# The first input tiles over two DMA queues, the turn of tile 1 and the parameter vectors in the opening of a fused scan and feed-forward kernel

## The chip, the core and the metric

The kernel runs on one core of a Trainium2 chip. The metric is the device time of one execution in microseconds (us). The core has five engines that run their own instruction streams and meet at semaphores: TensorE (PE, with its weight loads listed apart as PEld), VectorE (DVE), ScalarE (ACT), GpSimd (POOL) and SyncE (SP). Transfers between the device memory and the core's own memory are issued by SP or ScalarE and carried by 16 DMA engines.

## What is computed

```python
x  = A_x                       # 1 x 2048 x 512, bf16
xn = layernorm(x)
s  = S5(xn)                    # a complex diagonal recurrence over 2048 steps, 512 states
g  = silu((gelu(xn @ w_gate) * (xn @ w_up)) @ w_down)    # inner width 1376
out = x + s * g

# S5: Lam_bar = exp(exp(log_dt) * (Lambda_re + i Lambda_im))
#     h[t] = Lam_bar * h[t-1] + B_bar @ xn[t];  y = 2 Re(C h) + xn * Dskip
```

The three vectors `log_dt`, `Lambda_im` and `Lambda_re` (512 values each) give the rotation angles, the decay `rho` and the complex coefficients that are folded into C.

## The kernel before, in words

The 2048 rows are worked in four slabs of 512 rows, each of four tiles of 128 rows (tile m of slab s). For each slab: normalise, turn the rows so that the 512 features lie on partitions (`xnT`), multiply with `w_up` (wu) and `w_gate` (wg) and form gelu(gate) * up, turn that product (`at_t`), multiply with `w_down` (wd); beside it the scan: multiply with B, rotate, scan, rotate back, multiply with C. `y_tile` joins the two and writes the output.

The order of the work is not worked out at run time. Every piece of work is a numbered step, given with its engine, a planned cost and what it reads and writes (`Plan.add`, line 57); the tuple `ORDER` (line 21) lists all step numbers in the order in which they are emitted. The order of the steps of one engine in that tuple is the order in which that engine works; the planned costs and due times are left over from the planner that made it and do nothing in the kernel.

The opening, slab 0, is a special case. Three things are wanted early: x, the weights wu, and the three vectors.

- `load_x` (line 221) loads one tile of x, 128 rows of 1 KB, on SP's queue. Tiles 0, 1 and 2 come first, then the first 1024 columns of wu in four pieces by rows (`load_w`, k = 0 to 3), wu's last 352 columns, tile 3 of x, wg in two pieces, then wd's last rows, slab 1, Dskip. The issues on SP stand in this order. Behind them on SP come the DMA transposes (`dma_t4`, line 363, at L364; B, L237; `at_t`, L465) with wd's main load (L684) between them.
- The three vectors (lines 254 to 257) are loaded on ScalarE's queue, behind a dummy activation, into two small tiles `pv0` and `pv1`.
- `dummies` and `fill` (lines 296 to 303) are matmuls on constants, before any data are there: seven of 512 columns, then 256 columns at two places.
- `center(m)` (line 334) takes the mean of tile m and subtracts it. For tile 0 the sum is split: VectorE sums 384 columns (L341), ScalarE 128 (L339), and VectorE subtracts both (L343). For tiles 1 and 2 ScalarE sums (L347) and VectorE subtracts (L348).
- `head_t(m)` (line 305) turns a tile with four TensorE transposes (L313 for tile 0, L328 for tiles 1 and 2), and copies the result out of PSUM to `xcT` (in the buffer W): tile 0 in two halves, on VectorE (L319) and ScalarE (L321), tiles 1 and 2 in one copy on VectorE (L330).
- `up_rows(m, k)` (line 380) is the first product: for tile m and row block k of wu, two matmuls of 512 columns (L388) that add up over k in two PSUM banks. After k = 3 ScalarE scales the result by the rows' factor `rs` and takes it out (`out_up`, L398). `first_w` (line 406, L418) does the other products of slab 0.
- `stats`, `squares` and `rstd` (lines 277, 351, 285) find the factor `rs` of each tile; the power is taken on GpSimd (L292). `scale0` (line 355, L360 and L357) scales the turned-to-be rows; the DMA transposes of slab 0 read them.
- `parameters` (line 599) turns `pv0` and `pv1` with two small transposes (L603, L604), copies 12 columns out on VectorE (L606), then GpSimd takes the power dt (L607) and later rho (L611). `angles` (line 613) works out the angles on VectorE (L614 to L618) and sine and cosine on ScalarE (L619, L620). `coefficients` (line 703, L708 to L726) and `tables` (line 622, L639) follow on VectorE.

In the order before, TensorE's first steps are: dummies, fill, the turn of tile 0 in two halves, fill, the turn of tile 1, the two parameter transposes, then `up_rows` (0, 0), the turn of tile 2, (1, 0), (1, 1), (0, 1), (2, 0), (2, 1), (0, 2), (1, 2), (0, 3), (1, 3), (2, 2), (2, 3), and `first_w`. GpSimd's are: iotas and the identity, dt, the factors of tiles 1, 0, 2 and 3, a copy of the sine, rho, a copy of the cosine.

Of the kernel before, what the change touches and what calls it, by code (L numbers as in the profile page):

```python
# [80 lines left out]
def kernel(  # L81
# [18 lines left out]
    P = 128  # L100
# [37 lines left out]
    pv0, pv1 = sb("pv0", [4, P]), sb("pv1", [8, P])  # L138
# [82 lines left out]
    def load_x(m, end, landed):  # L221
        dma_sp(end, landed, lambda: nc.sync.dma_start(out=x_tok[:, m, :], in_=x_r[:, m, :]), [("x", 0, m)])

    W2 = CH[1][1]
    load_x(0, 1.12, 2.92)
    load_x(1, 1.59, 3.35)
    load_x(2, 2.06, 3.75)
    load_w("wu", 0, 1, 0, W2, 2.53, 5.1)
    load_w("wu", 1, 2, 0, W2, 3.0, 6.3)
    load_w("wu", 2, 3, 0, W2, 3.5, 7.4)  # L230
    load_w("wu", 3, 4, 0, W2, 4.0, 7.9)
    load_w("wu", 0, KT, W2, F, 4.5, 9.2)
    load_x(3, 5.0, 9.6)
# [71 lines left out]
    def head_t(m):  # L305
# [20 lines left out]
        def f():  # L326
            for k in range(KT):
                T.transpose(tp[:, k, :], xn[m][:, k * P : (k + 1) * P], ident[:])  # L328
# [516 lines left out]
```

## Time and profile before

| | us |
|---|---|
| median of 3 runs | 178.52 (178.51, 178.52, 178.72) |
| span of the profiled execution, first to last instruction | 176.3 |
| median less span | 2.2 |
| first product on wu (start) | 5.00 |
| first `first_w` product (start) | 10.39 |

The profile gives no time of its execution beside the span. Rows of the profile are read so: a timeline row has the start and the length in us, the engine, the line of the kernel, the operation, what it writes and reads, its shape and how many instructions were merged; in brackets the idle time before it and what ended it. A chain row has start, length, engine, tile and line. A DMA issue row has the tile, the queue, the count, KB each, and us from issue to landing. A row of a stretch has the stretch, its length, busy us and count of PE, PEld, DVE, ACT and POOL, the granted TensorE clock, the share of the DMA engines and GB/s.

### The profile page before, as it was taken

Reading aid. Unit: us, or ns where it says so; the run is one execution under the profiler, and the core shown is the slowest. Engines: PE = TensorE matmul, PEld = TensorE weight load, DVE = VectorE, ACT = ScalarE, POOL = GpSimd, SP = SyncE. Lnnn points to the kernel's source line nnn. Section 1 sums busy time; section 2 is a strip of 40 time slices with the busy share of each in tenths; the row PEclk is TensorE's granted clock in tenths of the full one; section 3 lists DMA queues with packets and bytes.
Section 4 is the critical chain, followed back from the end, with each engine's and each line's share of the span. In section 5 each row is a group of like instructions: output and inputs, shape, how many; then the busy total and the mean of one; then the engine's idle time right before and its main releaser. Section 6 shows DMA issues by size and latency. Waiting matters only on the chain.

```text
span 176.3 us, 2421 instructions
## 1 busy us (share of the span) xinstructions
PE 172.3 (98%) x847; PEld 82.3 (47%) x847; DVE 156.9 (89%) x252; ACT 123.5 (70%) x236; POOL 11.2 (6%) x25
## 2 busy tenths in 40 slices
PE   8999999999999999999999999999999999999992
PEld 2555454444454544444455454444444455444451
DVE  3859999999699984999979999899999999999764
ACT  6599979969999999799588845383058518482240
POOL 2660030000200000000040000000000000000000
PEclk9999999999999999999999999999999999999999
DMA  5999999998000809422000084194000007627112
GB/s 156 322 371 225 205 226 260 219 279 137 0 0 12 188 20 192 95 75 46 0 0 6 30 137 95 41 182 86 0 0 0 0 30 162 65 41 154 45 58 76
DMA packets 48355, 18.66 MB, mean 106 GB/s; under 512 B 40312, under 2 KB 47832, under 8 KB 48344
## 3 DMA queue, kind: packets, MB, share of 16 engines
q1 hardware_dynamic: 48320, 18.52, 48.8%
q8 instruction: 6, 0.10, 0.3%
q14 instruction: 5, 0.04, 0.1%
q10 hardware_dynamic: 24, 0.00, 0.0%
HBM read 6.46 MB, written 2.10 MB: 49 GB/s over the span
## 4 chain that ended last, share of the span: by engine, by line
PE 97%; DVE 1%; issue 0%; DVEq 0%
PE ring L449 32%; PE ring L481 22%; PE ring L547 16%; PE ybank L497 15%; PE ring L418 5%; PE ring L388 3%; PE ybank L418 2%; PE ring L299 1%; DVE yg L502 1%; PE ybank L299 1%; DVE junk L508 1%; PE ybank L328 0%; PE ring L303 0%; PE ring L313 0%; PE ring L603 0%
## 5 line engine op out<-in xcount | busy, mean ns | idle before, releaser
L449 PEld LDWEIGHTS <-xnT 128*128 128x128 bf16 x288 | 28.2, 98 | 28.4
L481 PE MATMUL ring<-wd,atT 128*128 128x512 bf16 (+1 forms) x176 | 39.3, 379 | 0.0
L449 PE MATMUL ring<-wg,xnT 128*128 128x512 bf16 (+1 forms) x144 | 31.6, 357 | 0.0
L449 PE MATMUL ring<-wu,xnT 128*128 128x512 bf16 (+1 forms) x144 | 31.3, 357 | 0.0
L547 PE MATMUL ring<-xnT,BT 128*128 128x512 bf16 x128 | 30.1, 379 | 0.0
L578 DVE TENSOR_TENSOR_SCAN Fs<-rho,ini,W 128x512 bf16<-128x512 f32 x24 | 29.7, 1271 | 0.1
L452 ACT ACTIVATE ub<-ring 128x512 bf16<-128x512 f32 (+1 forms) x36 | 19.2, 555 | 13.8 <-PE ring L449 13.7
L497 PE MATMUL ybank<-C,hst 128*128 128x512 bf16 x120 | 27.7, 379 | 0.0
L481 PEld LDWEIGHTS <-atT 128*128 128x128 bf16 (+1 forms) x176 | 17.2, 97 | 20.9
L549 ACT ACTIVATE U<-ring 128x512 bf16<-128x512 f32 x32 | 18.1, 599 | 7.5 <-PE ring L547 7.5
L452 ACT ACTIVATE gt<-ring 128x512 bf16<-128x512 f32 (+1 forms) x36 | 19.5, 556 | 3.7 <-PE ring L449 3.5
L497 PEld LDWEIGHTS <-hst 128*128 128x128 bf16 x136 | 13.3, 98 | 14.0
L484 ACT ACTIVATE g<-ring 128x512 f32<-128x512 f32 x16 | 9.4, 594 | 14.3 <-PE ring L481 14.2
L547 PEld LDWEIGHTS <-BT 128*128 128x128 bf16 x128 | 12.5, 97 | 14.8
L559 DVE TENSOR_TENSOR Q<-U,tab 128x4096 bf16<-128x4096 bf16 x8 | 18.3, 2289 | 0.9 <-ACT tab L646 0.7
L559 DVE TENSOR_TENSOR Q<-Fs,tab 128x4096 bf16<-128x4096 bf16 x8 | 18.3, 2288 | 0.1
L502 DVE TENSOR_TENSOR yg<-ybank,g 128x512 bf16<-128x512 f32 x15 | 10.2, 685 | 5.8 <-PE ybank L497 5.7
L763 ACT ACTIVATE junk<-x_tok 128x512 bf16<-128x512 bf16 x16 | 10.0, 632 | 1.2 <-DMA x_tok<-in_A_x_dram 1.2
L493 ACT ACTIVATE ybank<-sk 128x512 f32<-128x512 bf16 x15 | 9.1, 605 | 1.7 <-DVE yg L502 1.6
L768 ACT ACTIVATE xna<-x_tok,nb,rs 128x512 bf16<-128x512 bf16 x12 | 9.5, 812 | 0.0
L578 DVE TENSOR_TENSOR_SCAN Fs<-rho,W 128x512 bf16<-128x512 f32 x8 | 9.3, 1210 | 0.1
L458 DVE TENSOR_TENSOR at<-gt,ub 128x1024 bf16<-128x1024 bf16 x12 | 8.2, 683 | 0.0
(140 smaller groups left out, 169.7 us busy)
## 6 DMA issues: line engine op xcount, KB each, us to landing
x_tok<-in_A_x_dram SPq DMA_DIRECT2D x3, 512.0 KB, 4.6
out_dram<-ot SPq DMA_DIRECT2D x12, 128.0 KB, 1.8
wd<-in_B_w_down_dram SPq DMA_DIRECT2D x1, 1280.0 KB, 7.1
wu<-in_B_w_up_dram SPq DMA_DIRECT2D x4, 256.0 KB, 3.9
wg<-in_B_w_gate_dram SPq DMA_DIRECT2D x1, 864.0 KB
x_tok<-in_A_x_dram SPq DMA_DIRECT2D x4, 128.0 KB, 2.1
wg<-in_B_w_gate_dram SPq DMA_DIRECT2D x1, 512.0 KB, 6.0
wu<-in_B_w_up_dram SPq DMA_DIRECT2D x1, 352.0 KB, 5.3
```

Of the source, the lines that this page charges most:

```text
L418: T.matmul(ps[:, 0 : b - a], lhsT=lhs(k), rhs=wt[:, k, a:b], start=(k == 0), stop=(k == KT - 1))
L449: T.matmul(ps[:, 0 : b - a], lhsT=xnT[:, s % 2, m, k, :], rhs=wt[:, k, a:b], start=(k == 0), stop=(k == KT - 1))
L452: acts(b - a, lambda: act(out=dst[:, a:b], in_=ps[:, 0 : b - a], func=AF.Copy if up else AF.Gelu_apprx_tanh), [("bank", r)], [key], table= ...
L481: T.matmul(ps[:], lhsT=atT[:fs, k, m * P : (m + 1) * P], rhs=wd[:fs, k, :], start=(k == 0), stop=(k == NFT - 1))
L497: T.matmul(ps, lhsT=hst[s % 2][:, j // NPT, j % NPT, m * P : (m + 1) * P], rhs=C2[:, j // NPT, j % NPT, c0:c1], start=(j == 0 and not seed ...
L502: dve(w, lambda: V.tensor_tensor(out=yg[e][:, c0:c1], in0=ps, in1=g2[gi][:, b, c0:c1], op=ALU.mult), [key, ("g2", gi, b)], [("yg", e, c0)])
L547: T.matmul(ps[:], lhsT=BT[:, ri, k, pt * P : (pt + 1) * P], rhs=xnT[:, s % 2, :, k, :], start=(k == 0), stop=(k == KT - 1))
L549: acts(512, lambda q=q, ri=ri, ps=ps: act(out=U[ui][:, ri, q, :], in_=ps[:], func=AF.Copy), [("bank", r)], [("U", ui, q, ri)])
L559: dve(4096, lambda: V.tensor_tensor(out=Qf, in0=src.unsqueeze(1).to_broadcast(WQ), in1=table, op=ALU.mult), reads, ["Q"], rate=2.0)
L578: pl.add(DVE, 1.12 if s == 0 else 1.185, lambda ri=ri, q=q, pt=pt, first=first: V.tensor_tensor_scan(out=Fs[:, ri, q, :], data0=rho[:, pt ...
L763: acts(512, lambda i=i, fn=fn, sc=sc, m=m: act(out=junk()[:], in_=x_tok[:, s * M + m, :], func=fn, scale=sc, accum_out=sx[:, s, i, m : m + ...
L768: acts(512, lambda m=m: act(out=xn[m], in_=x_tok[:, s * M + m, :], func=AF.Identity, scale=rs[:, s, m : m + 1], bias=nb[:, s, m : m + 1]), ...
```

## The change

Loads. Of x's tiles 0 and 1, rows 0 to 63 are loaded on SP's queue and rows 64 to 127 on ScalarE's; tile 2 is loaded on ScalarE's queue whole. So wu k = 0 stands third on SP's queue and no longer fourth. The three vectors move from ScalarE's queue to SP's, behind wu k = 3 and ahead of wu's last columns; they land in one tile `pv` of 128 x 128, zeroed by VectorE first.

Tile 0. VectorE sums 320 columns and ScalarE 192; the centring is done in two halves.

Turns. The four transposes of tiles 1 and 2 write two PSUM banks, and their copies are split: VectorE takes the first half, ScalarE the second.

Parameters. One matmul of `pv` with 12 columns of the identity takes the place of the two transposes. In the code and in the order it stands later.

Order. TensorE: six dummies (seven before), fill, the turn of tile 0, fill, the turn of tile 1, `up_rows` (0, 0), (1, 0), (0, 1), the turn of tile 2, (1, 1), (2, 0), (2, 1), (0, 2), the parameters, (1, 2), (2, 2), (0, 3), (1, 3), (2, 3), then as before. GpSimd: the factor of tile 0, dt, the factors of tiles 1, 2 and 3, then as before. VectorE: the copy of the parameters stands behind tile 0's statistics, and the angles behind the scaling of tile 0, with tile 3's statistics between them. ScalarE: sum of tile 1, copy of tile 0, sum of tile 2, copies of tiles 1 and 2, the squares; sine and cosine both stand behind the first four `out_up`.

Output. Tiles 0 and 1 of the last slab are written with one transfer each instead of two.

The rest of `ORDER` is the same sequence with other numbers.

```diff
-    def load_x(m, end, landed):
-        dma_sp(end, landed, lambda: nc.sync.dma_start(out=x_tok[:, m, :], in_=x_r[:, m, :]), [("x", 0, m)])
+    def load_x(m, end, landed, p0=0, p1=P):
+        dma_sp(end, landed, lambda: nc.sync.dma_start(out=x_tok[p0:p1, m, :], in_=x_r[p0:p1, m, :]), [("x", 0, m)])
+    PH = P // 2
+    for m, p0, p1 in ((0, PH, P), (1, PH, P), (2, 0, P)):
+        if m < 2:
+            load_x(m, 1.0 + 0.25 * m, 2.6 + 0.3 * m, 0, PH)
+        dma(ACT, 0.4, 1.7, lambda m=m, p0=p0, p1=p1: A.dma_start(out=x_tok[p0:p1, m, :], in_=x_r[p0:p1, m, :]), writes=[("x", 0, m)], rank=900.0)
-    load_x(0, 1.12, 2.92)
-    load_x(1, 1.59, 3.35)
-    load_x(2, 2.06, 3.75)
...
+    dve(64, lambda: V.memset(pv[:], 0.0), writes=[("pv", i) for i in range(3)], rank=900.0)
...
     load_w("wu", 3, 4, 0, W2, 3.2, 6.8)
+    for i, v in enumerate((A_log_dt, A_Lambda_im, A_Lambda_re)):
+        dma_sp(3.6 + 0.4 * i, 6.0, lambda i=i, v=v: nc.sync.dma_start(out=pv[4 * i : 4 * i + 4, :], in_=v.rearrange("(k p) -> k p", p=P)), [("pv", i)])
     load_w("wu", 0, KT, W2, F, 4.9, 8.2)
...
-        bank, key = ybank[(m + 1) % 2], ("y", (m + 1) % 2)
-        tp = bank[:].bitcast(BF16)[:, 0:D].rearrange("p (k t) -> p k t", t=P)
+        banks = [(ybank[i], ("y", i)) for i in range(2)] if m == 1 else [(ring[2 + i], ("bank", 2 + i)) for i in range(2)]
+        tps = [b[:].bitcast(BF16)[:, 0 : D // 2].rearrange("p (k t) -> p k t", t=P) for b, _ in banks]
...
-        dve(512, lambda: V.tensor_copy(out=xcT[:, :, m * P : (m + 1) * P], in_=tp), [key], [("xcT", m, 0), ("xcT", m, 1)], rate=2.0, rank=310.0 - 20 * m)
+        dve(256, lambda: V.tensor_copy(out=xcT[:, 0:2, m * P : (m + 1) * P], in_=tps[0]), [banks[0][1]], [("xcT", m, 0)], rate=2.0, rank=310.0 - 20 * m)
+        acts(256, lambda: act(out=xcT[:, 2:4, m * P : (m + 1) * P], in_=tps[1], func=AF.Copy), [banks[1][1]], [("xcT", m, 1)], rank=310.0 - 20 * m)
...
-            c = 3 * P
+            c = 320
...
-        cuts = (0, HD) if (NS - 1, 0) <= (s, m) < (NS - 1, M - 2) else (c0,)
...
-            T.transpose(pt_ps[:, 0:4], pv0[:, :], ident[0:4, 0:4])
-            T.transpose(pt_ps[:, 4:12], pv1[:, :], ident[0:8, 0:8])
+            T.matmul(ybank[0][:, 0:12], lhsT=pv[:], rhs=ident[:, 0:12], start=True, stop=True)
...
-    dummies(7, 3)
+    dummies(6, 3)
```

More of the change, by code (lines that the diff above doesn't have):

```diff
@@ L137 @@
     C2 = sb("C2", [P, 2, NPT, D])
-    pv0, pv1 = sb("pv0", [4, P]), sb("pv1", [8, P])
+    pv = sb("pv", [P, P])
     Drow = sb("Drow", [P, D])
@@ L243 @@
     mhalf = small("mhalf", M)
-    tiny = small("tiny", 1)
     e_t = small("e_t")
@@ L251 @@
         early.append(dve(32, lambda i=i: V.memset(at[i][:, F:FP], 0.0), writes=[("atpad", i)], rank=900.0))
-    one = nc.const_aps.tensor(1.0, [P, 1], FP32)
-    first = [acts(1, lambda: act(out=tiny[:], in_=one, func=AF.Silu), [], ["tiny"], rank=910.0, not_before=0.72)]
-    for i, (t, v) in enumerate(((pv0[0:4, :], A_log_dt), (pv1[0:4, :], A_Lambda_im), (pv1[4:8, :], A_Lambda_re))):
-        first = [dma(ACT, 0.48, 1.7, lambda t=t, v=v: A.dma_start(out=t, in_=v.rearrange("(k p) -> k p", p=P)),
-                     writes=[("pv", i)], rank=900.0, not_before=0.8, after=first)]
     iota_i = sb("iota_i", [P, NBA], I32)
@@ L322, in head_t @@
             return
[L323 to L324 removed]
+        banks = [(ybank[i], ("y", i)) for i in range(2)] if m == 1 else [(ring[2 + i], ("bank", 2 + i)) for i in range(2)]
+        tps = [b[:].bitcast(BF16)[:, 0 : D // 2].rearrange("p (k t) -> p k t", t=P) for b, _ in banks]
         def f():
             for k in range(KT):
[L328 to L330 removed]
+                T.transpose(tps[k // 2][:, k % 2, :], xn[m][:, k * P : (k + 1) * P], ident[:])
+        pe(KT, P, f, [("xc", m, 0), ("xc", m, 1), "ident"], [key for _, key in banks])
+        dve(256, lambda: V.tensor_copy(out=xcT[:, 0:2, m * P : (m + 1) * P], in_=tps[0]), [banks[0][1]], [("xcT", m, 0)], rate=2.0, rank=310.0 - 20 * m)
+        acts(256, lambda: act(out=xcT[:, 2:4, m * P : (m + 1) * P], in_=tps[1], func=AF.Copy), [banks[1][1]], [("xcT", m, 1)], rank=310.0 - 20 * m)
     head, sums0 = [], []
@@ L342, in center @@
                                            accum_out=ma[:, 0:1]), [("x", 0, 0)], [("yg", 0, 0), ("ma", 0)], base=0.15, rank=400.0, after=early)
-            head.append(dve(512, lambda: V.tensor_scalar(out=xn[0], in0=x, scalar1=ma[:, 0:1], scalar2=mb[:, 0:1], op0=ALU.subtract, op1=ALU.subtract),
-                            [("x", 0, 0), ("ma", 0), "mb"], [("xc", 0, 0), ("xc", 0, 1)], rate=2.3, rank=400.0, after=head[-1:]))
+            for i in range(2):
+                hc = slice(i * HD, (i + 1) * HD)
+                head.append(dve(256, lambda hc=hc: V.tensor_scalar(out=xn[0][:, hc], in0=x[:, hc], scalar1=ma[:, 0:1], scalar2=mb[:, 0:1], op0=ALU.subtract, op1=ALU.subtract),
+                                [("x", 0, 0), ("ma", 0), "mb"], [("xc", 0, i)], rate=2.3, rank=400.0, after=head[-1:]))
             return
@@ L510, in y_part @@
         mg = s * TS + m * P
-        cuts = (0, HD) if (NS - 1, 0) <= (s, m) < (NS - 1, M - 2) else (c0,)
-        for lo, hi in zip(cuts, (*cuts[1:], c1)):
-            dma(SP, 0.35, 1.5, lambda lo=lo, hi=hi: nc.sync.dma_start(out=out_td[mg : mg + P, lo:hi], in_=ot[o][:, lo:hi]), [("ot", o, c0)], [("out", s, m, lo)], svc=(2, 0.4, 0.9))
+        dma(SP, 0.35, 1.5, lambda: nc.sync.dma_start(out=out_td[mg : mg + P, c0:c1], in_=ot[o][:, c0:c1]), [("ot", o, c0)], [("out", s, m, c0)], svc=(2, 0.4, 0.9))
     def y_tile(s, m):
@@ L599, in parameters @@
     def parameters():
-        pt_ps = ring[2][:].bitcast(BF16)
         def f():
-            T.transpose(pt_ps[:, 0:4], pv0[:, :], ident[0:4, 0:4])
-            T.transpose(pt_ps[:, 4:12], pv1[:, :], ident[0:8, 0:8])
-        pe(2, 60, f, [("pv", i) for i in range(3)] + ["ident"], [("bank", 2)])
-        dve(12, lambda: V.tensor_copy(out=pf[:], in_=pt_ps[:, 0:12]), [("bank", 2)], [("pf", 0), ("pf", 1)], rank=245.0)
+            T.matmul(ybank[0][:, 0:12], lhsT=pv[:], rhs=ident[:, 0:12], start=True, stop=True)
+        pe(1, 60, f, [("pv", i) for i in range(3)] + ["ident"], [("y", 0)])
+        dve(12, lambda: V.tensor_copy(out=pf[:], in_=ybank[0][:, 0:12]), [("y", 0)], [("pf", 0), ("pf", 1)], rank=245.0)
         pool(1.15, lambda: G.tensor_tensor(out=dt_[:], in0=e_t[:], in1=ldt, op=ALU.pow), [("pf", 0), "e_t"], ["dt"], rank=245.0)
@@ L654 @@
     fill(256, 3)
-    parameters()
     for m in range(1, M - 1):
@@ L660 @@
     stats(0)
-    angles()
     rstd(0, 1)
@@ L675 @@
             up_rows(m, k)
+    parameters()
+    angles()
     for m in range(M - 1):
```

16 lines of the change are left out of this document (9 added, 7 removed), and 46 rows, old and new, of the table ORDER.

## The prediction

> **What bounds the kernel now.** I read the page's busy shares first, then the chain of waits in order of time.
>
> ```profile
> span 176.3 us, 2421 instructions
> PE 172.3 (98%) x847; PEld 82.3 (47%) x847; DVE 156.9 (89%) x252; ACT 123.5 (70%) x236; POOL 11.2 (6%) x25
> ```
> ```profile
> 1.77 2.13 PE ring L299 x5
> ...
> 4.50 0.40 PE ybank L328 x4
> 4.90 0.11 PE ring L603
> ...
> 5.03 0.55 PE ring L388 x2
> ...
> 5.81 4.75 PE ring L388 x22
> ...
> 166.13 5.20 PE ybank L497 x24
> ```
>
> Columns of the chain are start, length, and what holds it. From 5.03 to 171.3 us every piece is TensorE and the next begins where the last ends. So the end of the kernel is the start of the first product plus fixed work, and the change is worth what it does to that start, unless it opens a hole later. The profiled span is 176.3 us; the median run is 178.52, so 2.2 us lie around the span, which the change doesn't touch. The timeline of TensorE gives instruction starts, which I use from here on:
>
> ```profile
> 5.00 0.59 PE L388 MATMUL ring<-wu,W 128*128 128x512 bf16 x2
> ...
> 5.65 4.91 PE L388 MATMUL ring<-wu,W 128*128 128x512 bf16 x22
> 10.39 1.36 PE L418 MATMUL ybank<-wu,W 128*128 128x352 bf16 x8
> ```
>
> The opening stage is 24 matmuls and the turn of tile 2. 22 of them take 10.39 − 5.65 = 4.74, so 0.216 each and 0.43 for a step of two; the turn takes 5.65 − 5.00 − 0.43 = 0.22. What decides 5.00? The timeline of the other engines, and the issues with their time from issue to landing (one query for each issue; x's tile 0, then wu's rows k = 0 to 3):
>
> ```profile
> 0.72 1.34 SPq L222 DMA_DIRECT2D x_tok<-in_A_x_dram  x3
> 2.11 2.33 SPq L213 DMA_DIRECT2D wu<-in_B_w_up_dram  x5
> ```
> ```profile
> x_tok<-in_A_x_dram SPq DMA_DIRECT2D x1, 128.0 KB, 2.1
> ```
> ```profile
> wu<-in_B_w_up_dram SPq DMA_DIRECT2D x1, 256.0 KB, 2.8
> ```
> ```profile
> wu<-in_B_w_up_dram SPq DMA_DIRECT2D x1, 256.0 KB, 3.3
> ```
> ```profile
> wu<-in_B_w_up_dram SPq DMA_DIRECT2D x1, 256.0 KB, 4.5
> ```
> ```profile
> wu<-in_B_w_up_dram SPq DMA_DIRECT2D x1, 256.0 KB, 4.8
> ```
> ```profile
> 2.85 0.55 DVE L341 TENSOR_SCALAR_CACHE_REDUCE yg<-x_tok 128x384 bf16<-128x384 bf16 x1 [1.82 <-DMA x_tok<-in_A_x_dram]
> ...
> 3.33 0.63 ACT L347 ACTIVATE junk<-x_tok 128x512 bf16<-128x512 bf16 x1
> ...
> 3.52 0.41 DVE L343 TENSOR_SCALAR xna<-x_tok,ma,mb 128x512 bf16<-128x512 bf16 x1
> ...
> 4.09 0.35 DVE L348 TENSOR_SCALAR xna<-x_tok,ma 128x512 bf16<-128x512 bf16 x1 [0.16 <-ACT junk L347]
> 4.36 0.28 DVE L319 COPY W<-ring 128x256 bf16<-128x256 bf16 x1
> ```
>
> SP issues one transfer each 0.46 us ((2.11 − 0.72) / 3). Tile 1 is issued at 1.18 and lands at about 3.3, where its sum on ScalarE starts (3.33); centring follows at 4.09, its turn at 4.50, the two parameter transposes, then the product. On the other side wu's first rows land at 2.11 + 2.8 = 4.9. **Two things end together at 5.00**: the turn of tile 1 with the parameters behind it, and the landing of wu k = 0. Later rows land at 2.58 + 3.3 = 5.9, 3.06 + 4.5 = 7.6 and 3.53 + 4.8 = 8.3. Their first users start at 6.08 (two matmuls after 5.65), 7.81 (ten) and 8.67 (fourteen): margins of 0.2 to 0.4 us.
>
> **The change, part by part.** *x in halves.* Tiles 0 and 1 go out as 64 rows on SP and 64 on ScalarE, tile 2 on ScalarE alone.
>
> ```profile
> 0.79 0.55 ACTq L256 DMA_DIRECT2D pv<-in_A_log_dt_dram  x1
> ```
>
> ScalarE's first issue starts 0.07 after SP's and holds its queue 0.55, so the upper half of tile 1 goes out near 1.34 against 1.18 for the whole tile now. A half on two queues is not in the trace. Bounds for landing: 0.2 us earlier (the data of half a tile), 0.2 later (ScalarE's later issue). I take tile 0 at 0.05 and tile 1 at 0.05 earlier. The split of tile 0's sum (320 columns on VectorE, not 384: 0.55 × 64/384 = 0.09 less) and the centring in two halves get tile 0 turned some 0.2 sooner, but its copy (L319) stays behind tile 1's centring on VectorE, which waits for ScalarE's sum: nothing is gained there. The memset of pv and the six instead of seven warming matmuls lie ahead of the data, in idle time (VectorE waits 1.82 before 2.85).
>
> *Turn of tile 1, then the product.* Both orders turn tile 1 first; what goes from between are the parameters. Turn at 4.45, plus 0.22: the product could start at T = 4.68. I take 4.70.
>
> *wu moves up one place on SP*, 0.46 earlier. But the same 640 KB have to pass before its first rows are in. A table of stretches shows how full the DMA engines are:
>
> ```profile
> 1.70:2.50 0.80, 0.80 (x4) 0.24 (x3) 0.00 (x0) 0.50 (x2) 0.19 (x1) 1.00 0.82 200
> 2.50:3.40 0.90, 0.90 (x4) 0.34 (x3) 0.55 (x2) 0.47 (x3) 0.00 (x0) 1.00 0.91 265
> 3.40:5.00 1.60, 1.60 (x15) 0.68 (x14) 1.25 (x6) 1.60 (x6) 0.00 (x0) 1.00 0.92 284
> 5.00:8.00 3.00, 3.00 (x19) 1.49 (x18) 2.53 (x11) 1.36 (x4) 2.10 (x5) 1.00 1.01 326
> ```
>
> The last two columns are the DMA share and GB/s. Until 5.0 a tenth or so lies open; after that nothing does. If x and wu ran at 326 from 1.7 on, 655 kB would take 2.0 us, against 2.6 to 2.7 at the three rates shown: bounds of 0 and 0.6 earlier. I take the middle, 0.3: rows land at 4.6, 5.6, 7.3 and 8.0.
>
> *The new order of products* is tile 0, 1, 0 (k = 1), turn of tile 2, tiles 1, 2, 2, tile 0 (k = 2), parameters, and the rest. Split copies (VectorE and ScalarE, a bank each) let a product follow its turn after one step of two: 0.28 for the copy against 0.43, hidden. One matmul of 12 columns for the parameters: between one transpose's 0.22/4 = 0.06 and the present 0.11; I take 0.06. The stage then ends at the latest of four: T + 24 × 0.216 + 0.22 + 0.06 = T + 5.46 = 10.16; wu k = 1, needed 0.86 after T, so 5.6 + 4.60 = 10.2; wu k = 2, needed 2.81 after T, so 7.3 + 2.65 = 9.95; and the parameters, needed 3.24 after T (7.94), so their landing + 2.22.
>
> *Parameters on SP behind wu k = 3.* They can't land before those rows' share on the same engines: as early as hidden (7.2), as late as 8.0 + 0.1. I take 8.0, which gives 10.22. wu's last columns and tile 3 are issued some 1 us later, behind three small issues; DMA share 1.01 says the queue is full then, so this is hidden; without that cover it would be that 1 us, less their margins.
>
> So the stage ends at **10.22 instead of 10.39: 0.17 us gained**.
>
> *What is late next.* The parameters also feed a chain on GpSimd and VectorE:
>
> ```profile
> 5.57 1.03 POOL L607 TENSOR_TENSOR dt__136<-e_t,pf 128x4 f32<-128x4 f32 x1 [3.68 <-DVE pf L606]
> ```
> ```profile
> 10.68 0.23 POOL L289 TENSOR_SCALAR ve<-mv 128x1 f32<-128x1 f32 x1 [1.14 <-DVE mv L281]
> 11.00 0.55 POOL L292 TENSOR_TENSOR rs<-ve,mhalf 128x1 f32<-128x1 f32 x1
> 11.51 0.29 POOL L627 CAST sh<-sbt 128x128 bf16<-128x128 f32 x1
> 11.76 1.11 POOL L611 TENSOR_TENSOR rho<-e_t,a 128x4 f32<-128x4 f32 x1
> ```
> ```profile
> 12.90 0.23 DVE L708 TENSOR_TENSOR nre<-rho,cbt 128x4 f32<-128x4 f32 x1 [0.90 <-POOL rho L611]
> ```
>
> Now dt starts at 5.57 and three scale factors follow in its slack. In the new order dt starts near 8.6 (matmul at 7.95, copy, then behind tile 0's factor), ends at 9.6, and tiles 1, 2 and 3 follow at about 0.9 each (10.68 to 11.55): 12.4 instead of 11.55. rho and the coefficients move with it: 12.90 becomes 13.8. VectorE already waits 0.90 there; I count no idle time behind it that would catch this up, so its tables come 0.9 late too. SP waits for tile 3's scaling before its transposes, and wd's load is queued behind them:
>
> ```profile
> 12.03 3.60 SPq L364 DMA_TRANSPOSE xnT<-xna  x2
> ...
> 22.37 0.93 SPq L684 DMA_DIRECT2D wd<-in_B_w_down_dram  x1
> ```
> ```profile
> wd<-in_B_w_down_dram SPq DMA_DIRECT2D x1, 1280.0 KB, 7.1
> ```
> ```profile
> 30.87 7.13 PE ring L481 x33
> ```
>
> wd lands at 22.37 + 7.1 = 29.5 and is used from 30.87 in the chain, which runs 0.16 behind the starts (5.81 against 5.65): 1.2 us of slack. 0.9 late and TensorE 0.17 early leaves 0.1 to 0.2. Hidden, barely. The output of two late tiles in one transfer instead of two isn't in the last tiles' path: nothing.
>
> Forecast: 178.52 − 0.17 = **178.35**.
>
> **The rivals.** *DMA fills at once (faster).* If halves on two queues close the open tenth, wu lands 0.5 to 0.6 earlier and T, with tile 1 at 3.1, is 4.5: the stage ends at 9.95 to 10.0, gain 0.4, 178.1. For: 0.82 and 200 GB/s at the start. Against: tile 1's upper half is issued later than the whole is now.
>
> *Parameters late (slower).* If wu k = 3 comes no sooner than 8.3 on the engines that carry the parameters, these land at 8.4: TensorE, in order, stands from 7.94, the stage ends at 10.62 (+0.23), dt starts at 8.9 or later and wd is 1.3 to 1.4 late, another 0.2 of stall: 178.9 to 179.0. It decides from a landing of 8.17 on, where the stage is no earlier than now. For: k = 2 and 3 need 4.5 and 4.8 us from issue, against 2.8 for k = 0; a full queue stands ahead of any small transfer. Against: only four of the engines' shares matter.
>
> *Halves buy nothing.* Both halves share the same engines; x lands as now or 0.1 later and wu k = 1 at 5.9, but it is needed 0.2 sooner in the new order: 5.9 + 4.60 = 10.5, 178.6. For: the DMA share is already 0.9.
> [...]
>
> *The clock.* Two fills in the timeline:
>
> ```profile
> 3.70 0.42 PE L303 MATMUL ring<-const-bfloat16-1.0 128*128 128x256 bf16 x1
> ...
> 4.23 0.27 PE L303 MATMUL ring<-const-bfloat16-1.0 128*128 128x256 bf16 x1
> ```
>
> The same matmul takes 0.42 and then 0.27; warming matmuls run at 2.13 / 5 = 0.43, products at 0.216. The pace doubles between 3.70 and 4.23, after 3 us of steady work. Six warming matmuls and the fill end near 3.5, and TensorE then idles 0.2 to 0.3 before the first turn. If that puts the doubling off by another 2 to 3 us past 4.7, half of it is lost: 1.0 to 1.5, 179.7. Against: the work also began only at 0.76.
> [...]
>
> **How the numbers follow.** Forecast 0.29 (0.23 within 0.2%, 0.06 faster); DMA fills at once 0.18 (0.16 faster, 0.02 within); parameters late 0.31 (0.25 slower, 0.06 within); halves buy nothing 0.14 (0.10 within, 0.04 slower); clock 0.08 slower. 0.2% is 0.36 us, about what a measurement of this kernel can tell from no change. Faster 0.22, same 0.41, slower 0.37. The range, 177.95 to 179.3, takes in the ends of the first four and leaves out the clock; the forecast alone is 178.1 to 178.6.
>
> **What would show it.** First product near 4.70 and not 5.00; k = 1 rows landing by 5.6; the first 352-column product near 10.2; dt at 8.6, coefficients at 13.8, wd's first use with no wait. I'm wrong if TensorE waits at the parameter matmul, if a second pace shows after 4.7, or if a hole opens between 18 and 35 us.

## The result and the profile after

The changed kernel takes 180.77 us (median of 14 executions, 178.60 to 181.34); the kernel before, beside it on the same chip, 178.65 (178.43 to 179.22, 14 executions). The ratio is 1.0084, 95% interval 1.0064 to 1.0104: by the medians **slower by 2.1 us** where 178.35 was forecast, outside the range. The ratios leave out executions more than 1.5% above the fastest of the same kernel (two of these fourteen, and four of ten when the kernel after ran again as e12, the profiled one among them), so that 1.0084 is 1.5 us where the medians differ by 2.1. Four of the fourteen took 178.60 to 179.46; the profile below is not of one of these, and what they were spared isn't known.

The head of the profiled execution (180.35 us):

```profile
span 178.6 us, 2409 instructions
...
PE 171.5 (96%) x829; PEld 81.8 (46%) x845; DVE 156.8 (88%) x254; ACT 124.0 (69%) x238; POOL 11.3 (6%) x25
```

TensorE is busy no longer than before (171.5 against 172.3) in a span that is 2.3 longer, so what was lost is time in which it stands idle. The timeline of TensorE shows the first part of that, its waits the second (columns of the waits: engine, what is waited for, us in all, times, longest):

```profile
4.27 0.54 PE L315 MATMUL ring<-ident,xna 128*128 128x128 bf16 x4 [0.58 <-DVE xna L348]
...
5.38 0.40 PE L330 MATMUL ybank<-ident,xna 128*128 128x128 bf16 x4 [0.46 <-DVE xna L353]
5.61 1.48 PE L393 MATMUL ring<-wu,W 128*128 128x512 bf16 x6
...
8.89 0.17 PE L604 MATMUL ybank<-ident,pv 128*128 128x12 bf16 x1
...
11.07 1.36 PE L423 MATMUL ybank<-wu,W 128*128 128x352 bf16 x8
```
```profile
PE ring L486 <- DMA wd<-in_B_w_down_dram: 1.2, 1, 1.2
```

The first product starts at 5.61 (5.00 before), the first product of 352 columns at 11.07 (10.39): **0.68 late**. Then wd is not there: a wait of 1.2 us; between the starts of the matmuls around it 1.4 us are missing. 0.68 + 1.4 is 2.1 of the 2.3; the rest are small waits. Which work stands behind both is in the chain of waits:

```profile
1.36 2.77 DMA x_tok<-in_A_x_dram
4.21 0.73 ACT junk L352 x2
4.97 0.36 DVE xna L353
5.38 0.40 PE ybank L330 x4
...
9.35 1.03 POOL dt__135 L607
...
11.26 0.61 DVE st L282
...
13.69 1.08 POOL rho L611
...
21.33 0.60 DVE at L436
...
23.81 1.16 SPq L470
25.02 7.96 DMA wd<-in_B_w_down_dram
33.02 2.10 PE ring L486 x9
```

Before, this chain ran on TensorE alone from 5.03 on. Now it starts with the upper half of x's tile 1 on ScalarE's queue (issued 1.36, landed 4.13), goes by way of its sum, centring and turn into the first product, and later leaves TensorE: dt, tile 3's statistics, rho, the tables, a transpose on SP, and wd's load behind it. The DMA issues of the first 12 us (columns: tile and queue, count, KB each, median us from issue to landing) and SP's timeline:

```profile
x_tok<-in_A_x_dram SPq DMA_DIRECT2D x2, 64.0 KB, 2.1
x_tok<-in_A_x_dram ACTq DMA_DIRECT2D x2, 64.0 KB, 2.8
x_tok<-in_A_x_dram ACTq DMA_DIRECT2D x1, 128.0 KB, 3.1
```
```profile
0.72 1.21 SPq L222 DMA_DIRECT2D x_tok<-in_A_x_dram  x2
1.98 2.00 SPq L213 DMA_DIRECT2D wu<-in_B_w_up_dram  x4
4.09 0.31 SPq L240 DMA_DIRECT2D pv<-in_A_log_dt_dram  x1
4.95 0.25 SPq L240 DMA_DIRECT2D pv<-in_A_Lambda_im_dram  x1
...
6.09 0.42 SPq L213 DMA_DIRECT2D wu<-in_B_w_up_dram  x1
...
9.26 1.12 SPq L686 DMA_DIRECT2D Drow<-in_A_Dskip_dram  x1
13.92 3.53 SPq L369 DMA_TRANSPOSE xnT<-xna  x2
...
25.02 0.73 SPq L684 DMA_DIRECT2D wd<-in_B_w_down_dram  x1
```
```profile
SPq L213 <- DMA wu<-in_B_w_up_dram: 0.5, 1, 0.5
SPq L240 <- DMA wu<-in_B_w_up_dram: 0.5, 1, 0.5
```

A half on SP takes as long to land as a whole tile did (2.1 us), the upper half of tile 1 on ScalarE's queue 2.8. SP now holds still inside the loads: the second parameter row until wu k = 0 has landed (4.93), wu's last columns until wu k = 1 has landed (6.07). The operands of the transfers in the trace show why: in both kernels they take turns on eight semaphores (S103 to S110), over both queues together, and each load that came to a semaphore again was issued after its last user, six to ten issues earlier, had landed (4.95 after 4.93, 6.09 after 6.07). Before, ten transfers stood ahead of wu's last columns, which shared a semaphore with x's tile 2 (landed 3.88) and didn't wait; now twelve do, and the partner is wu k = 1 (6.07). They go out at 6.09 instead of 4.01, and the last load, Drow, lands at 17.59 instead of 15.67. The DMA engines, at a share of 1.01 from 5.0 to 8.0 us before, are no longer full there:

```profile
5.00:8.00 3.00, 2.62 (x18) 1.28 (x19) 1.93 (x6) 1.88 (x6) 0.00 (x0) 1.00 0.81 258
```

Two theories came of this, and a third later. **F**: halves don't bring x sooner; each costs a longer issue (0.58 us on SP, 0.40 for a whole tile before) and lands like a whole tile. **D**: the two more transfers run into the eight semaphores, the loads end late, and what follows on SP, wd last of all, is late too. The rival to D, **P**: the parameters' later chain on VectorE and GpSimd holds SP up by itself. **G**: TensorE's idle stretches ahead of the first product decide when its full pace comes.

### The profile page after: what moved, and what is told of

Same layout as the page of the kernel before. It is cut to its first block, busy times and chain, and to the rows that moved or that the text cites. A ratio compares the mean times of both kernels' runs of the same rounds, so it can differ in the third digit from the quotient of the medians.

```text
span 178.6 us, 2409 instructions
## 1 busy us (share of the span) xinstructions
PE 171.5 (96%) x829; PEld 81.8 (46%) x845; DVE 156.8 (88%) x254; ACT 124.0 (69%) x238; POOL 11.3 (6%) x25
## 4 chain that ended last, share of the span: by engine, by line
PE 79%; DVE 8%; DMA 6%; POOL 2%; issue 1%; ACT 1%; SPq 1%; DVEq 0%; ACTq 0%
PE ring L454 31%; PE ring L486 21%; PE ybank L502 14%; PE ring L550 12%; DMA wd<-in_B_w_down_dram 4%; DVE st L282 2%; DMA x_tok<-in_A_x_dram 2%; DVE Q L639 1%; DVE yg L507 1%; PE ring L393 1%; SPq L470 1%; POOL rs L294 1%; DVE mv L283 1%; DVE tab L639 1%; POOL rho L611 1%
## 5 line engine op out<-in xcount | busy, mean ns | idle before, releaser
L552 ACT ACTIVATE U<-ring 128x512 bf16<-128x512 f32 x32 | 18.1, 599 | 7.5 <-PE ring L550 7.5
```

Source lines behind the costliest of these rows:

```text
L552: acts(512, lambda q=q, ri=ri, ps=ps: act(out=U[ui][:, ri, q, :], in_=ps[:], func=AF.Copy), [("bank", r)], [("U", ui, q, ri)])
```

## The experiments

All are the kernel after with the edit that the text gives; e6, e7 and e11 are the kernel before with one; e12 is the kernel after itself. The last five columns come from one execution of each. "Hole" is the time missing between the starts of the matmuls around wd's first use; Drow's landing is the end of the opening loads.

| kernel | median (range), executions | before beside it | ratio, 95% | span profiled | first product | first of 352 | wd lands | hole |
|---|---|---|---|---|---|---|---|---|
| e1_x_whole | 179.75 (178.93 to 180.12), 10 | 178.74 | 1.0061, 1.0041 to 1.0081 | 177.9 | 4.96 | 11.34 | 32.19 | 0.6 |
| e2_tile3_first | 180.20 (178.64 to 181.26), 10 | 178.74 | 1.0076, 1.0037 to 1.0115 | 179.5 | 5.83 | 11.39 | 33.40 | 1.2 |
| e3_halves_one_queue | 182.32 (181.4 to 183.3), 4 | 178.74 | 1.0213, 1.0144 to 1.0281 | 179.7 | 6.64 | 13.25 | 34.06 | 0.5 |
| e4_two_queues_whole | 180.15 (178.83 to 181.56), 4 | 178.74 | 1.0116, 1.0024 to 1.0208 | 177.0 | 5.53 | 10.97 | 31.30 | 0.1 |
| e5_loads_as_before | 178.96 (178.30 to 180.67), 10 | 178.79 | 1.0029, 0.9998 to 1.0060 | 176.9 | 4.88 | 10.91 | 30.72 | 0 |
| e6_only_halves | 183.44 (182.47 to 184.06), 4 | 178.79 | 1.0234, 1.0159 to 1.0309 | 181.2 | 7.58 | 15.05 | 32.80 | 0 |
| e7_three_more_loads | 179.22 (178.46 to 180.86), 10 | 178.79 | 1.0016, 0.9980 to 1.0053 | 176.7 | 5.07 | 10.48 | 30.75 | 0 |
| e8_wu0_ahead_of_x2 | 179.05 (178.62 to 180.43), 10 | 178.79 | 1.0012, 0.9977 to 1.0047 | 177.8 | 5.04 | 11.59 | 31.92 | 0.1 |
| e9_seven_fills | 179.26 (178.42 to 180.26), 8 | 178.53 | 1.0032, 1.0009 to 1.0056 | 178.5 | 5.63 | 11.35 | 32.65 | 1.0 |
| e10_no_parameter_loads | 179.66 (179.27 to 179.95), 4 | 178.53 | 1.0060, 1.0037 to 1.0083 | 177.9 | 5.62 | 11.09 | 31.81 | 0.45 |
| e11_six_fills | 178.52 (178.12 to 179.11), 10 | 178.53 | 1.0006, 0.9991 to 1.0021 | 176.6 | 5.37 | 10.78 | 30.38 | 0 |
| e12_after_again | 181.25 (178.84 to 182.51), 10 | 178.53 | 1.0097, 1.0058 to 1.0136 | 180.7 | 5.84 | 13.41 | 35.12 | 1.4 |
| e13_more_fills | 179.53 (178.92 to 180.88), 10 | 178.73 | 1.0043, 1.0019 to 1.0067 | 178.1 | 5.30 | 10.85 | 32.49 | 0.95 |
| e14_loads_before_tile3_first | 178.66 (178.22 to 179.19), 10 | 178.73 | 0.9990, 0.9958 to 1.0022 | 176.5 | 4.97 | 10.47 | 30.66 | 0 |
| e15_wd_early | 183.20 (182.27 to 184.39), 4 | 178.73 | 1.0246, 1.0191 to 1.0300 | 180.5 | 6.29 | 13.28 | 22.03 | 0 |

### The halves: e1, e3, e4, e6

e1 loads tiles 0 to 2 whole on SP and leaves the rest of the change:

```diff
-    for m, p0, p1 in ((0, PH, P), (1, PH, P), (2, 0, P)):
-        if m < 2:
-            load_x(m, 1.0 + 0.25 * m, 2.6 + 0.3 * m, 0, PH)
-        dma(ACT, 0.4, 1.7, lambda m=m, p0=p0, p1=p1: A.dma_start(out=x_tok[p0:p1, m, :], in_=x_r[p0:p1, m, :]), ...)
+    for m in range(3):
+        load_x(m, 1.0 + 0.25 * m, 2.6 + 0.3 * m)
```

> The changed kernel with x's tiles 0, 1 and 2 loaded whole on SP's queue again, in the order of before; all else as changed. Theory S (the second queue makes x late: in the changed kernel tiles 0 and 1 land at 3.14 and 4.13 us, before at 2.83 and 3.31): tiles land at 2.8, 3.3 and 3.9, the first product starts at 4.75 to 5.0 instead of 5.61, the first 352-column product at 10.3 to 10.5 instead of 11.07; the parameter chain starts 0.6 earlier, so wd's load too, and the hole of 1.5 us ahead of the down products shrinks to 0.5 to 0.9: 178.9 to 179.4. Rival C (the late parameters are all of the loss, the loads count for nothing): the hole stays at 1.5 us and the time above 180.3.

The first product is back at 4.96, so its 0.6 us belong to the way x is loaded (F). But wu k = 1 landed only at 6.72 in this execution, so that the first product of 352 columns came at 11.34, not at 10.5 or sooner, and the time is 179.75, above what was expected. The waits show both losses:

```profile
PE ring L393 <- DMA wu<-in_B_w_up_dram: 0.8, 1, 0.8
PE ring L486 <- DMA wd<-in_B_w_down_dram: 0.4, 1, 0.4
```

e3 puts both halves on SP's queue, and tile 2 too; e4 keeps two queues with whole tiles (0 and 2 on SP, 1 on ScalarE):

```diff
e3  +        load_x(m, 1.0 + 0.25 * m, 2.6 + 0.3 * m, p0, p1)      # upper half: SP as well
e4  +        if m != 1: load_x(m, ...)                             # whole
e4  +        else: dma(ACT, ..., A.dma_start(out=x_tok[:, m, :], in_=x_r[:, m, :]), ...)
```

> The changed kernel with the same halves of tiles 0 and 1, but all of x on SP's queue (lower half, upper half, tile after tile, then tile 2), nothing on ScalarE's. Theory S (the second queue is what makes x late): two more issues of about 0.4 us each stand ahead of tile 1 and wu; tile 0 lands at 2.9 to 3.1, tile 1 at 3.6 to 3.9, sooner than the 4.13 of the changed kernel; first product 5.0 to 5.4. Rival H (halving itself makes x late, small transfers moving as slowly on any queue): tile 0 at 3.2 or later, tile 1 at 4.1 or later, first product at 5.6 or later.

> The changed kernel with x in whole tiles, tile 1 on ScalarE's queue and tiles 0 and 2 on SP's. Theory S: with both queues issuing at once each issue takes 0.55 us or more (0.40 alone), and tile 1, though issued at 0.78, lands no sooner than 3.3, as it did third of a kind on one queue; tile 0 at 2.9 to 3.1; first product 4.8 to 5.2. Rival H (only halves are slow, two queues in themselves are a gain): issues of 0.40, tile 1 lands by 3.0, first product by 4.7 or held by wu alone.

SP's timeline in e3:

```profile
0.72 3.12 SPq L222 DMA_DIRECT2D x_tok<-in_A_x_dram  x5
3.89 1.85 SPq L213 DMA_DIRECT2D wu<-in_B_w_up_dram  x4
```

The rival H holds: tile 0 is whole at 3.49 and tile 1 at 4.78. The five pieces of x take 3.17 us of SP, 0.63 each, against 0.46 for a whole tile before, and the halves land 2.1 to 2.2 us after their issue. It isn't the size of the piece alone that costs: the fifth piece is a whole tile and took 0.59 to issue too, as wu k = 0 did behind the halves in the kernel after (0.58); the transfer behind these took 0.42 again. Why is open. In e4 the issues on the two queues stay at 0.37 to 0.41 us though they run side by side, and tiles 0, 1 and 2 land at 2.97, 3.16 and 3.49, the last two earlier than before (3.31, 3.88). So the second queue alone doesn't make x late; with the cut it came late. It brings no gain either: wu k = 0, issued at 1.64, landed at 5.49, later than before (4.95), and the first product came at 5.53 (4.96 in e1). Two executions of e4 took 178.8 to 179.0 and two 181.3 to 181.6; the profile is of a quick one, and what cost the others is open.

e6 is the kernel before with tiles 0 and 1 in halves, the parameters behind the upper halves on ScalarE's queue:

```diff
+    def upper(i):
+        for m in range(2 if i == 0 else 0):
+            A.dma_start(out=x_tok[P // 2 : P, m, :], in_=x_r[P // 2 : P, m, :])
```

> The kernel before with only tiles 0 and 1 of x in two halves, the lower on SP, the upper on ScalarE's queue ahead of the parameters; nothing else is changed. Theory F (a half takes 0.58 us to issue where a whole tile takes 0.40, and lands no sooner after its issue): tile 0 complete at about 3.1, tile 1 at about 4.1 (before: 2.83 and 3.31), first product at 5.5 to 5.8 instead of 5.00, first product of 352 columns at about 11.0 instead of 10.4, time 179.2 to 179.5. Rival (the halves are harmless and the kernel after lost only through its parameters and its new order): first product within 0.1 us of 5.0, time within 0.2 us of the kernel before.

The tiles landed as expected (3.16 and 4.01), but the time is far over, for two other reasons: the first product came at 7.58, and then half pace, of which more below, cost 2.1 us (7.5 instead of 5.4 until the first product of 352 columns). ScalarE's timeline shows the first:

```profile
3.02 0.27 ACTq L261 DMA_DIRECT2D pv<-in_A_Lambda_im_dram  x1
4.35 0.26 ACTq L261 DMA_DIRECT2D pv<-in_A_Lambda_re_dram  x1
4.65 0.31 ACT L344 ACTIVATE junk<-x_tok 128x128 bf16<-128x128 bf16 x1 [2.44 <-DMA x_tok<-in_A_x_dram]
```

The third parameter row was issued at 4.35, when the load that had its semaphore last (tile 2, 4.33) had landed. ScalarE can't sum tile 0, there since 3.16, before it has issued that load. The row names x as the releaser, but x had long landed. This is D's mechanism on a queue that belongs to an engine with work; the run says nothing on what F costs alone.

### The loads' order and the parameters: e2, e5, e7, e8, e10

e2 changes only `ORDER`: tile 3's statistics, factor and scaling ahead of the angles on VectorE and GpSimd.

> The changed kernel with one change of order: tile 3's statistics on VectorE ahead of the angles, its scale factor on GpSimd ahead of tile 2's, and its scaling ahead of tiles 1 and 2, so that SP's transposes no longer stand behind the parameters. Loads as changed. Theory P (wd is late because SP's queue waits for tile 3's scaling behind the parameter chain): SP's first transpose is issued at 12.8 instead of 13.92, wd's main load about 1.1 earlier (23.9 instead of 25.02), the hole ahead of the down products falls from 1.5 to 0.5 or less: 179.6 to 179.9 against 180.7 for the changed kernel. Rival V (the hole is set by VectorE's tables and the turned gate product, which come as late as before): the hole stays above 1.2 and the time within 0.3 us of the changed kernel.

As far as P goes by way of tile 3's scaling, it falls as the only cause: the first transpose went out 0.7 earlier (13.25), yet wd no earlier, the hole stayed, and the time, 180.20, is above what was expected. In this run the loads end at 18.1, and the transpose landed at 18.6, behind them.

e5 keeps the change's order but loads x whole on SP and the parameters early on ScalarE's queue:

```diff
+    def load_pv(*ii):
+        if 0 in ii:
+            V.memset(pv[:], 0.0)
+        for i in ii:
+            A.dma_start(out=pv[4 * i : 4 * i + 4, :], in_=vecs[i].rearrange("(k p) -> k p", p=P))
+    for m in range(3):
+        load_x(m, 1.0 + 0.25 * m, 2.6 + 0.3 * m)
+        if m < 2:
+            dma(ACT, 0.4, 1.7, lambda m=m: load_pv(*((0,), (1, 2))[m]), ...)
```

> The kernel after with x's tiles 0 to 2 whole on SP and the three parameter rows on ScalarE's queue at the start, as before; the split centring, the turn of tile 1 ahead of the first product, its evictions on two engines, the parameters' product behind wu's rows and the new order stay. Theory D (at most eight transfers are under way; two more halves and three parameter loads on SP make SP wait for landings, and the tail of the loads comes late): wu's last columns are issued at about 4.0 us instead of 6.09, Drow lands at about 15.7 instead of 17.6, wd lands at 29.5 to 30.2, no hole in TensorE's row at 33 us, first product at about 4.9 to 5.0, time 178.5 to 178.8. Rival P (the later chain of the parameters itself holds up what comes after it): 179.4 or more, with a hole of 0.5 us or more at the first use of wd.

wu's last columns went out at 4.01, Drow landed at 15.52, and the hole is gone. **Most of the loss is in where the loads stand:** what is left is 0.2 us by the medians, 0.5 by the ratio, between 0 and 1.1 by its interval. The first product of 352 columns is still at 10.91, not 10.39: three products of wu ran at 0.38 to 0.43 each instead of 0.22, half pace. That gave theory G.

e7 is the kernel before with three extra small loads into scratch between wu k = 3 and wu's last columns:

```diff
+        for i, v in enumerate((A_log_dt, A_Lambda_im, A_Lambda_re)):
+            nc.sync.dma_start(out=pvx[4 * i : 4 * i + 4, :], in_=v.rearrange("(k p) -> k p", p=P))
```

> The kernel before with three loads more, of 1 KB to 1.5 KB each, into scratch that nothing reads, on SP between wu's fourth row and wu's last columns; the parameters stay where they are. Theory D: the third of them waits for the landing of wu's first row (4.95), wu's last columns are issued at about 5.2 instead of 4.01, Drow lands at about 16.7 instead of 15.7, wd some 1 us later than 29.5 (to 30.5), which its slack of about 1.2 us just takes up: time 0 to 0.3 us above before. Rival (the queue is full, so later issues are hidden): Drow and wd land within 0.2 us of before.

SP's timeline:

```profile
4.88 0.25 SPq L236 DMA_DIRECT2D pvx<-in_A_Lambda_re_dram  x1
5.17 0.41 SPq L213 DMA_DIRECT2D wu<-in_B_w_up_dram  x1
```

Within 0.3 us as expected, against the rival: the third waits for wu k = 0 (4.86), wu's last columns go out at 5.17, Drow lands at 16.47, wd at 30.75, 1.25 later than before, and its slack just takes it up.

e8 is e5 with wu k = 0 ahead of x's tile 2 in `ORDER`.

> The kernel with loads as before (x whole, parameters on ScalarE's queue, the new order), with wu's first row issued ahead of x's third tile: wu's first row lands at about 4.5 instead of 4.95, x's third tile at about 4.4 instead of 3.9. If the landing of wu's first row sets the first product: first product at about 4.75 and a time 0.1 to 0.3 us below the kernel that it is made from. If x's third tile or the turns set it: no gain or a loss of up to 0.3 us.

wu k = 0 landed at 4.76, but tile 2 at 5.10 and wu k = 1 at 6.97, and TensorE waited 0.9 for the latter: no gain.

e10 takes the three parameter loads out of the kernel after and sets their tile to a constant, so that it computes with other state matrices:

```diff
-        dma_sp(..., lambda i=i, v=v: nc.sync.dma_start(out=pv[4 * i : 4 * i + 4, :], in_=...), [("pv", i)])
+        dma_sp(..., lambda: None, [("pv", i)])
```

> The kernel after without its three loads of the parameter rows: the tile they would fill is set to a constant on VectorE, so the state matrices are those of other parameters; the halves, both queues and the order stay. Theory D (the three loads on SP, with the two more halves, make SP wait for landings): wu's last columns are issued at about 4.1 us instead of 6.09, Drow lands at about 15.7 instead of 17.6, wd at 30 to 31, no hole at 33 us or one under 0.3; the first product stays at about 5.6 (theory F, that is the halves'), the first product of 352 columns at about 11.0; time 178.9 to 179.3. Rival (the halves alone hold up the loads and the transposes): wu's last columns still after 5.5, Drow after 17, a hole of over 0.8, time 180 or more.

The loads end at 15.83 as expected, but D is not all of it: the hole shrinks to 0.45 and the time to 179.66, not under 179.3. Its waits at wd:

```profile
PE ring L486 <- DMA wd<-in_B_w_down_dram: 0.3, 1, 0.3
```

The first transpose is still issued at 13.94, since tile 3 is scaled at 13.50. Set side by side, from the traces (the last column is the time from the first transpose's issue to wd's, in which SP issues one transfer after the other):

| kernel | Drow lands | tile 3 scaled | first transpose issued, landed | wd issued, landed | SP |
|---|---|---|---|---|---|
| before | 15.67 | 11.59 | 12.03, 16.29 | 22.37, 29.50 | 10.3 |
| after | 17.59 | 13.48 | 13.92, 18.08 | 25.02, 32.98 | 11.1 |
| e2 (scaling early, loads late) | 18.12 | 12.81 | 13.25, 18.60 | 25.47, 33.40 | 12.2 |
| e10 (loads early, scaling late) | 15.83 | 13.50 | 13.94, 16.46 | 24.84, 31.81 | 10.9 |
| e5 (loads early, scaling late) | 15.52 | 13.32 | 13.76, 16.34 | 23.85, 30.72 | 10.1 |
| e14 (both early) | 15.62 | 12.02 | 12.46, 16.25 | 22.98, 30.66 | 10.5 |

A late scaling starts SP's row of transposes late; late loads make it longer. The first transpose lands 0.5 to 0.65 us behind the last load, except where it went out so late (e5, e10) that it took 2.5 to 2.6 us from its own issue. Each of the two alone leaves wd later than before, by 1.2 us (e5) to 3.9 (e2); a hole is left in e2 and e10, none in e5. e10 and e5 agree in both conditions, so what sets their holes apart (0.45, none) is open.

### The pace: e9, e11, e12, e13

> The kernel with x whole on SP and the parameters on ScalarE's queue, with seven fill products of 512 columns at the start, as before, instead of six. Theory G (what is left of its lateness, a first product of 352 columns at 10.9 instead of 10.4, is three products at half pace, because TensorE stood idle for 0.3 us behind six fills): no product of wu over 0.25 us, the first product at about 5.0, the first product of 352 columns at about 10.4, time 178.5 to 178.8, that of the kernel before. Rival (the moment at which the full pace comes does not hang on the seventh fill): products of 0.4 us again after 4.9, and 10.7 or more.

```diff
-    dummies(6, 3)
+    dummies(7, 3)
```

e9 is e5 with the seventh fill, and G can't be judged by it. The pace was full, but x's tile 1 and wu k = 0 landed at 3.82 and 5.59 (in e5, with the same issues, 3.15 and 4.84), and the first product came at 5.63.

e11 is the kernel before with the opposite edit, seven to six.

> The kernel before with six fill products of 512 columns instead of seven, nothing else changed. Theory G: TensorE idles some 0.3 us before the turn of tile 0, the full pace comes after the first product instead of at 3.9 us, one to five products of wu take 0.43 instead of 0.215, the first product of 352 columns comes at 10.6 to 11.2 instead of 10.4, time 0.1 to 0.6 us over before. Rival: pace and time of the kernel before within 0.1 us.

The rival holds: no product ran at half pace, the time is that of before. The turns of tiles 0 and 1 did (0.107 for each transpose, not 0.056), so the full pace came later, just in time.

> The kernel after, unchanged, on the chip of the three others, for a second profiled execution. Theories D and F: wu's last columns issued at 5.9 to 6.3 us, Drow landed at 17 to 18, first product at 5.5 to 5.8, a hole at the first use of wd of 0.8 to 1.6 us, time 179.8 to 180.8. Rival (the first profile showed an unlucky execution): first product under 5.3 or no hole, and a time under 179.3.

The same kernel, and a different execution. Its timeline, and one stretch of each execution, the first one and then this one:

```profile
5.84 2.77 PE L393 MATMUL ring<-wu,W 128*128 128x512 bf16 x6
...
13.41 0.76 PE L423 MATMUL ybank<-wu,W 128*128 128x352 bf16 x4
```
```profile
5.60:10.50 4.90, 4.90 (x31) 2.22 (x28) 2.34 (x9) 2.81 (x9) 1.86 (x4) 1.00 0.91 271
```
```profile
5.60:10.50 4.90, 4.90 (x19) 2.27 (x18) 1.72 (x5) 2.42 (x7) 0.36 (x2) 1.00 0.87 260
```

Busy time (4.90) and granted clock (1.00) are the same; only the count tells: 31 matmuls against 19. Half pace lasted until 10.1: from the first product to the first of 352 columns it is 7.57 us instead of 5.46, so it cost 2.1, which is what the spans differ by. The holes (1.4) and late loads of the first profile are here too. e15, which opens as the kernel after does, shows half pace until 9.3 (20 matmuls in the same stretch). The idle stretches ahead of the first product are about as long here (0.60 and 0.29 us) as in the first execution (0.58 and 0.46), so they alone don't decide, and G isn't shown.

e13 fills TensorE's idle stretches:

```diff
-    dummies(6, 3)
+    dummies(8, 3)
-    fill(256, 3)                      # the one behind the turn of tile 0
+    pe(2, 384, lambda: [T.matmul(ring[3][:, 0:w], lhsT=warm[:, 0:P], rhs=warm[:, 0:w], start=True, stop=True) for w in (512, 256)], [], [("bank", 3)])
```

> The kernel after with more fill products ahead of the first product: eight of 512 columns at the start instead of six, and 512 and 256 behind the turn of tile 0 instead of 256, so that TensorE hardly idles from 0.8 us to the turn of tile 1. Theory G (TensorE's idle stretches of 0.8 and 0.5 us decide whether the full pace comes before the first product or 4 us later): all products of wu at 0.21 to 0.23 us, first product at 5.5 to 5.8, first product of 352 columns at 11.0 to 11.2, no execution above 180.8, median 179.8 to 180.4; the hole at wd stays at 0.8 to 1.5. Rival (the pace does not hang on the fills): times spread up to 181.5 or more as before, median 180.7 or more.

All products of wu ran at full pace. The median fell more than expected, to 179.53; in the profiled execution the upper half of tile 1 landed at 3.82, and whether it did so in the others isn't known. One execution of ten, 180.88, lies over the bound that was set. What is left is mostly wd:

```profile
PE ring L486 <- DMA wd<-in_B_w_down_dram: 0.8, 1, 0.8
```

### wd alone, and what the runs point to: e15, e14

e15 moves only wd's load in `ORDER`, ahead of the first two transposes.

> The kernel after with the load of wd's main part moved ahead of the two first transposes on SP instead of behind the first transpose of the product tiles; nothing else is changed. If the hole at the first use of wd is the wait for that load alone: wd lands by 20 to 22 us, no hole at 33 us, the executions at full pace 1.2 to 1.5 us shorter: the profiled span of such an execution at 177.1 to 177.4, median of all 179.0 to 179.9. Rival (the transposes are then late by wd's transfer, and TensorE waits for them instead): a hole of 1 us or more at the first use of the turned rows between 22 and 33 us, and no gain.

The rival holds: wd lands at 22.03, and the transposes wait in its place. TensorE's waits:

```profile
PE ring L550 <- DMA BT<-in_A_B_re_dram: 0.6, 1, 0.6
...
PE ring L423 <- DMA xnT<-xna: 0.4, 1, 0.4
```

Where these waits end, 0.7 and 0.45 us are missing between starts. Most of the rest stands ahead of them: the first product came at 6.29 (5.61 in the kernel after), and half pace cost 1.5 us.

e14 joins e5, the seven fills of e9 and the order of e2.

> The kernel with x whole on SP and the parameters early on ScalarE's queue, seven fills of 512 columns as before, and tile 3's statistics, factor and scaling ahead of the parameters' chain on VectorE and GpSimd. Theory: the first transpose is issued 1.9 us behind the first product of 352 columns instead of 2.9, the hole at wd is gone, no half pace: time 178.3 to 178.8, that of the kernel before; what is left of the change gains 0.2 us at most. Rival (the new order costs by itself): 179 or more, with a hole at wd of over 0.3.

SP's timeline and TensorE's only wait:

```profile
12.46 3.01 SPq L377 DMA_TRANSPOSE xnT<-xna  x2
...
22.98 0.78 SPq L692 DMA_DIRECT2D wd<-in_B_w_down_dram  x1
```
```profile
PE ring L401 <- DMA wu<-in_B_w_up_dram: 0.2, 1, 0.2
```

178.66 against 178.73: the loss is gone, and the rest of the change (turn of tile 1 first, split copies, one matmul for the parameters) gains nothing that can be measured, because wu k = 0 still lands at 4.93. No version beat the kernel before.

## Why the prediction was wrong, point by point

- **"I take tile 0 at 0.05 and tile 1 at 0.05 earlier", bounds of 0.2 either way: this failed, and T with it (5.61, not 4.70).** Tile 0 was whole at 3.14 instead of 2.83, tile 1 at 4.13 instead of 3.31, 0.8 late. The issue at 1.34 was right (1.36). What was missed is that its landing took 2.77 us and that half the data saves nothing: SP's halves took 2.1, as the whole tile did, and more to issue (0.58 against 0.40). Two queues with whole tiles don't make x late (e4); why the upper half took 2.77 and not 2.1 is open. In e3, with both halves on one queue, tile 0 is whole at 3.49, and the halves land 0.6 to 0.7 us apart, as they were issued. The rival "halves buy nothing" was right that both halves share the same engines (in the kernel after tile 0's lower half alone takes 0.72 of the 16 engines from 2.2 to 2.3 us, its upper half 0.77 from 2.5 to 2.6), but put the landing at "now or 0.1 later"; it was 0.8.
- **The sum of the stage** was right: T + 5.46; measured 11.07 − 5.61 = 5.46. So was the parameters' landing, 8.0 (8.05, behind wu k = 3 at 7.88), with no wait at their matmul, and the third and fourth rows of wu (7.3 and 8.0; 7.25 and 7.88). Not the first two: 4.93 and 6.07 instead of 4.6 and 5.6, no gain from one place up.
- **"Issued some 1 us later ...; DMA share 1.01 says the queue is full then, so this is hidden": failed.** They went out 2.1 us later, and the loads ended 1.9 later. The share that hid it belonged to the order before; over the same 5.0 to 8.0 us it is 0.81 in the kernel after. What the step lacked is the wait for the semaphore's last user, which turns two more transfers into a late issue. "Without that cover it would be that 1 us" was the right alternative, too small.
- **"dt starts near 8.6 ... 0.9 late", "hidden, barely": failed by size.** dt started at 9.35, 0.75 later than forecast and all of it from T, and tile 3's scaling came 1.9 late. The working counted GpSimd's chain, not that tile 3's statistics stand behind the angles on VectorE (11.26 in the chain); GpSimd itself had tile 2's factor until 12.29, so the two end together. SP then took 0.8 longer to reach wd, and wd's own landing 7.96 instead of the 7.1 counted. So wd landed 3.5 late; with 1.2 of slack, and needed 0.9 later, that leaves the 1.4 that were lost. The place, wd's first use, was named among what would show it wrong.
- **"Parameters late"** did not happen at its place, TensorE's parameter matmul; its second half, wd late, did. Its "only four of the engines' shares" shows in the marks that a landing leaves on its semaphore: four for `log_dt` (S104, 7.23 to 7.69), 16 for the lower half of tile 0 (S103, 2.67 to 2.85). **"DMA fills at once"** is refuted.
- **"The clock", 0.08:** half pace past 4.7 is real in the kernel after, in some executions, at 2.1 us, not 1.0 to 1.5. What sets its end isn't shown: the same kernel had its first product of 352 columns at 11.07 in one execution and at 13.41 in another. A later x made the first idle stretch 0.6 us and not the 0.2 to 0.3 assumed, but in both executions alike. How much of the median it carries stays open: the first profile explains its 2.3 us without it, e13 lowers the median by about 1 us with fills alone, and the landing of x differs between those runs too.

## What to carry to other kernels

Cutting a first load in halves to start sooner needs a trace in which landing time depends on size; where a half and a whole both land after 2.1 us, the cut only adds issues. Count the transfers ahead of the one that matters, on all queues, against the number of semaphores that they take turns on (eight here, S103 to S110), and ask what stands behind the one that waits, above all on an engine that computes (in e6 ScalarE began at 4.65 to sum a tile that was there at 3.16). A full DMA share before a change is no cover after it, since the change may itself open the gap (1.01 before, 0.81 after, from 5.0 to 8.0 us).

## What had not been expected of the hardware

- A 64-row half took 0.58 us to issue on SP, a whole tile 0.40; the second one on ScalarE's queue 0.84. A whole transfer right behind the halves took 0.58 to 0.59 too.
- The same loads issued at the same times land up to 0.75 us apart between executions: wu k = 0, issued at 2.11, at 4.84 (e5), 4.93 (e14) and 5.59 (e9).
- A busy share of 100% and a granted clock of 1.00 don't show TensorE's half pace: 31 against 19 matmuls in 4.9 us. Full pace came at about 3.9 us (before), 6.1 (e5) and 10.1 (e12), all with the first matmul at 0.76.
